# The second product of a dense FFN with slots stationary in a one-core attention, MoE and FFN kernel

## The chip, the cores and the metric

The kernel runs on one core of a Trainium2 chip. The metric is the device time of one execution in microseconds. Before and after are compared by the medians of several executions.

## The reference, cut to what matters

```python
def reference(...):
    attn_out = _attn_ref(q, k, v, omega)              # Performer features, 4 x 576 tokens, 8 heads of 64
    x = attn_out.transpose(0, 2, 1, 3).reshape(2304, 512)
    x = _moe_ref(x, expert_emb, tau, w1, w2)          # 8 experts, 512 -> 1024 -> 512
    return _moe2_ref(x, w_in, w_out)                  # the dense FFN

def _moe_ref(x, expert_emb, tau, w1, w2):
    ...
    expert_idx = np.argmax(logits, axis=1)
    gate_w = probs[np.arange(N), expert_idx]
    for e in range(E):
        mask = expert_idx == e
        h = np.maximum(x[mask] @ w1[e], 0.0)
        out[mask] = gate_w[mask, None] * (h @ w2[e])

def _moe2_ref(x, w_in, w_out):                        # 512 -> 2048 -> 512
    h = np.maximum(x @ w_in, 0.0)
    return h * h @ w_out
```

The gate is a positive number per token, and relu squared is of degree two, so the kernel applies the gate's square at the very end, to the rows of the output.

## The kernel before, in words

The work has three stages. The attention builds features of q and k, and writes the token rows x to DRAM. The MoE stage sorts the 2304 tokens by expert into 8 chunks of C = 290 slots, each of one expert: two chunks are filled from the first half of the tokens (`plan_a`), six once all tokens are there (`plan_b`). A plan builds one-hot matrices on VectorE (L726, L729, L732) and multiplies them on TensorE (L738) into a table: token numbers to gather from, token numbers to scatter to, and the gate. `gather` (L144) loads the 290 rows of a chunk by indirect DMA from GpSimd (L153) in three pieces of 128, 128 and 34 rows, transposes them on TensorE (L166) and splits them into two parts (L170, L171). Every product is done with three matmuls of split numbers (`mm3`, L185 to L189): high by high, high by low, low by high. `moe` (L252) runs a chunk: 8 blocks of hidden units, an `up` of 12 matmuls each, relu into h (ScalarE L262, VectorE L263), and with a lag of one block a `down` of 12 matmuls into four accumulators. The expert weights arrive by DMA as raw tiles (L222, L227), and `split` (L140 to L142) makes the two parts: ScalarE copies to the high part, VectorE or GpSimd subtracts for the low part. GpSimd does it for chunk 1, and for half of chunk 2. `keep` (L272) writes the chunk's result, transposed, into five column tiles yf.

The FFN (`ffn`, L306) takes the 2320 slots as NF = 5 tiles of W2 = 464 columns, and the 16 blocks of hidden units in four quarters of GF = 4. For each quarter, tile and block, `hidden` (L286) does an up of 12 matmuls, relu (L292), square (L294, L295) and a subtraction (L296) into g; two blocks later a `down` with the weights stationary and g as the moving operand adds into four accumulators of 128 outputs by 464 slots. At the end of four blocks VectorE adds them to oacc (L327, L329). In the last quarter, `finish` (L343) turns each finished chunk back: four transposes to a group of rows (L351), multiplication by the gate into an orow buffer (ScalarE L354, VectorE L356; three buffers), and an indirect scatter to the output from GpSimd (L357), 24 groups in all. The FFN's weights come as 64-bit numbers; `decode` (L104 to L118) makes them into fp32 with four operations of VectorE (L114 to L117) and splits them with GpSimd (L142). `prep_w` (L120) does it for the next quarter: the DMA (L112) and the decode go in while a quarter runs, into four buffers. A scheduler orders each engine's instructions from the traced program; each engine works strictly in that order.

Three more chunks of the kernel (`more`) run only if a token has no slot, and they do not run here. The end of the program waits for all scatters.

Of the kernel before, what the change touches and what calls it, by code (L numbers as in the profile page):

```python
# [24 lines left out]
NF, W2 = 5, 464  # L25
# [5 lines left out]
def kernel(  # L31
# [33 lines left out]
    RING, RAW, OROW = 4, 4, 1  # L65
# [3 lines left out]
    act = mctx.enter_context(tc.tile_pool(name="act", bufs=2))  # L69
# [5 lines left out]
    def columns(pool, js):  # L75
        for j in js:
            yf[j] = pool.tile([P, 2, KD, W2], F32R, name=f"yf{j}")
# [11 lines left out]
    tab = const.tile([P, 9 * (NA + NBMAX)], I32, name="tab")  # L89
    o = 0  # L90
    cuts = []
    for n in (3 * NA, 3 * NA, 3 * NA, 3 * NBMAX, 3 * NBMAX, 3 * NBMAX):
        cuts.append(tab[:, o:o + n])
        o += n
    gi_a, si_a, g2_a, gi_b, si_b, g2_b = cuts
    g2_a, g2_b = g2_a.bitcast(F32), g2_b.bitcast(F32)
# [7 lines left out]
    def decode(dst, src, kk, pool):  # L104
# [13 lines left out]
        split(dst, hi.bitcast(F32), nc.gpsimd)  # L118
# [14 lines left out]
    def cols(c):  # L133
        return (gi_a, si_a, g2_a, 3 * c) if c < NA else (gi_b, si_b, g2_b, 3 * (c - NA))

# [4 lines left out]
    def split(dst, src, eng=nc.vector):  # L140
        nc.scalar.copy(dst[:, 0], src)  # L141
        eng.tensor_sub(dst[:, 1], src, dst[:, 0].bitcast(F32))  # L142

    def gather(c, ahead=0):  # L144

        gi, _, _, col = cols(c)
        xt = act.tile([P, 2, KD, C], F32R, name="xt", tag="act")
        xT[c] = xt
        def load(t):
            n = ROWS[t][1]  # L150
            tag = dict(tag="row", bufs=2) if t < 2 or not ahead else dict(tag="orow", bufs=OROW)
            xg = s2.tile([P, DM], F32, name="xg", **tag)
            nc.gpsimd.indirect_dma_start(  # L153
                out=xg[:n], out_offset=None, in_=x_dram[:HALF] if c < NA else x_dram,
                in_offset=bass.IndirectOffsetOnAxis(ap=gi[:n, col + t:col + t + 1], axis=0),
            )
            return xg

        xgs = [load(t) for t in range(3 if ahead else 2)]
        for _ in range(ahead):  # L160
            yield
        for t, (r0, n) in enumerate(ROWS):
            xg = xgs.pop(0)
            p = px()
            for kk in range(KD):
                nc.tensor.transpose(p[:, kk * n:kk * n + n], xg[:n, kk * P:(kk + 1) * P], ident[:n, :n])  # L166
            if t == 0 and not ahead:
                xgs.append(load(2))
            pv = p[:, :KD * n].rearrange("p (k n) -> p k n", k=KD)
            nc.scalar.copy(xt[:, 0, :, r0:r0 + n], pv)  # L170
            nc.vector.tensor_sub(xt[:, 1, :, r0:r0 + n], pv, xt[:, 0, :, r0:r0 + n].bitcast(F32))  # L171
            yield
# [8 lines left out]
    def run(gen):  # L181
        for _ in gen:
            pass
# [46 lines left out]
    def feed(n):  # L230
        for _ in range(n):
# [9 lines left out]
            split(w, r, nc.gpsimd if c == 1 or (c == 2 and j) else nc.vector)  # L241
# [30 lines left out]
    def keep(c, acc):  # L272

        done = None
        for d in range(KD):
            s0 = c * C
            while s0 < (c + 1) * C:
                j, o = divmod(s0, W2)
                n = min((c + 1) * C - s0, W2 - o)
# [19 lines left out]
    def ffn_steps():  # L299

        for q0 in range(0, K2, GF):
            for j in range(NF):
                for i in range(GF):
                    yield q0, j, i

    def ffn():  # L306
        steps = list(ffn_steps())
        gs = {}
        acc = None
        for t in range(len(steps) + LAG2):  # L310
            if t:
                tick()
            if t < len(steps):
                q0, j, i = steps[t]
                gs[t] = hidden(q0 + i, yf[j])
            if t >= LAG2:
                q0, j, i = steps[t - LAG2]
                if i == 0:
                    acc = accumulators()
                down(acc, wout[q0 + i], gs.pop(t - LAG2), i, GF)  # L320
                last = None
                if i == GF - 1:
                    o = oacc[:, :, j * W2:(j + 1) * W2]
                    for d in range(KD):
                        if q0 == 0:
                            last = (nc.vector if d % 2 else nc.scalar)
                            last = last.tensor_copy(o[:, d], acc[d][:, :W2]) if d % 2 else last.copy(o[:, d], acc[d][:, :W2])  # L327
                        else:
                            last = nc.vector.tensor_add(o[:, d], o[:, d], acc[d][:, :W2])  # L329
                    if q0 == K2 - GF:  # L330
                        for c in range(NA + NB):
                            if j * W2 < (c + 1) * C <= (j + 1) * W2:
                                side.append(finish(c, oacc[:, :, c * C:(c + 1) * C]))

                q1 = q0 + GF
                if q1 < K2:
                    if j < NF - 1 and i == 1:
                        prep_w(q1 + j // 2, j % 2)
                    elif j == NF - 1 and i < GF - 2:
                        prep_w(q1 + 2 + i, 0)  # L340
                        prep_w(q1 + 2 + i, 1)
# [622 lines left out]
```

## Time and profile before

| what | value |
|---|---|
| median of 3 runs | 860.44 us |
| lowest and highest run | 854.92 and 863.81 us |
| the profiled execution | 855.59 us |
| its span, first to last instruction | 853.8 us |
| mean granted clock of TensorE | 0.985 |
| first FFN matmul | 412.23 us |
| last FFN matmul starts | 824.79 us |

All times below are in us from the start of the span. The clock is the share of full speed that TensorE was granted. Matmuls are pipelined: the duration of one overlaps the next, so what counts is how far apart their starts are. An engine that waits shows an idle time with what released it, in brackets.

### The profile page before, as it was taken

To read this page: it belongs to the slowest core of one execution; us is meant where nothing else is said; L and a number is where in the kernel's file an instruction comes from. 1 tells how busy PE (TensorE), PEld (TensorE's weight loads), DVE (VectorE), ACT (ScalarE), POOL (GpSimd) and SP (SyncE) were. 2 spreads that over 40 slices of the span, in tenths; PEclk is the share of its full clock that TensorE was granted. 3 is DMA by queue.
4 is the path that set the end of the run, shared out by engine and by line. 5 is a ranking of instruction groups with operands and counts; after the bars stand their busy time and mean duration, and the time that the engine had idled before them with its cause. 6 is when DMAs were issued, how large, how long until landed. Compare 5 with 4: busy or idle time off the path is not lost.

```text
span 853.8 us, 14040 instructions
## 1 busy us (share of the span) xinstructions
PE 812.6 (95%) x5118; PEld 750.7 (88%) x5118; DVE 511.9 (60%) x1115; ACT 361.6 (42%) x852; POOL 190.4 (22%) x217
## 2 busy tenths in 40 slices
PE   6999999998999999998999999999999999999981
PEld 6999998998989999998988888888888888888860
DVE  6777688688665788898333279333873343343430
ACT  5666787654355556554332243222322222222220
POOL 1133433533664221040000042000410011011133
PEclk9999999999999999998999999999999999999995
DMA  8334444366475776685000033000410000000111
GB/s 199 88 108 120 130 116 106 87 180 215 117 211 167 240 204 172 206 254 181 1 1 1 0 101 98 1 1 2 146 51 1 1 0 1 1 29 29 40 69 62
DMA packets 100927, 79.75 MB, mean 93 GB/s; under 512 B 29904, under 2 KB 88272, under 8 KB 100848
## 3 DMA queue, kind: packets, MB, share of 16 engines
q1 hardware_dynamic: 95728, 69.27, 28.3%
q0 software_dynamic: 5120, 9.49, 3.6%
q8 instruction: 42, 0.69, 0.3%
q14 instruction: 37, 0.30, 0.1%
HBM read 69.29 MB, written 9.47 MB: 92 GB/s over the span
## 4 chain that ended last, share of the span: by engine, by line
PE 71%; issue 14%; DVE 6%; DMA 3%; POOL 3%; ACT 1%; SPq 0%; POOLq 0%; ACTq 0%; DVEq 0%
PE pm L189 9%; PE pm L187 9%; PE pm L188 9%; PE acc L188 9%; PE acc L187 9%; PE acc L189 9%; PE pk L560 3%; DMA raw<-in_moe_w_dram 3%; PE pn L606 3%; POOL out_dram L357 2%; PE pp L537 2%; PE px L588 2%; PE pp L539 2%; PE pp L538 2%; PE px L516 2%
## 5 line engine op out<-in xcount | busy, mean ns | idle before, releaser
L292 ACT ACTIVATE r<-pm 128x464 f32<-128x464 f32 x80 | 44.7, 559 | 264.6 <-PE pm L189 264.6
L295 DVE TENSOR_TENSOR r<-r 128x464 f32<-128x464 f32 x80 | 54.8, 685 | 149.7 <-ACT r L292 149.7
L142 POOL TENSOR_TENSOR wf<-r,wf 128x512 fp32r<-128x512 f32 x32 | 51.3, 1613 | 336.7 <-ACT wf L141 310.6
L187 PE MATMUL pm<-yf,wf 128*128 128x464 f32 x320 | 120.0, 375 | 0.0
L187 PE MATMUL acc<-g,wf 128*128 128x464 f32 x320 | 119.6, 375 | 0.0
L189 PE MATMUL acc<-g,wf 128*128 128x464 f32 x320 | 119.4, 373 | 0.0
L189 PE MATMUL pm<-yf,wf 128*128 128x464 f32 x320 | 119.4, 373 | 0.0
L188 PE MATMUL pm<-yf,wf 128*128 128x464 f32 x320 | 119.2, 372 | 0.0
L188 PE MATMUL acc<-g,wf 128*128 128x464 f32 x320 | 118.9, 371 | 0.0
L141 ACT CAST wu<-raw 128x512 fp32r<-128x512 f32 x128 | 79.0, 622 | 70.2 <-PE acc L189 26.0
L142 DVE TENSOR_TENSOR wu<-raw,wu 128x512 fp32r<-128x512 f32 x104 | 82.1, 794 | 19.6 <-ACT wu L141 18.4
L187 PE MATMUL pm<-xt,wu 128*128 128x290 f32 x256 | 78.3, 306 | 2.9 <-DVE h L263 2.1
L189 PE MATMUL pm<-xt,wu 128*128 128x290 f32 x256 | 77.9, 304 | 2.5 <-DVE wu L142 2.5
L188 PE MATMUL pm<-xt,wu 128*128 128x290 f32 x256 | 76.8, 300 | 0.0
L188 PE MATMUL acc<-h,wu 128*128 128x290 f32 x256 | 71.4, 300 | 2.0 <-DVE h L263 2.0
L189 PE MATMUL acc<-h,wu 128*128 128x290 f32 x256 | 70.6, 295 | 0.0
L549 ACT ACTIVATE ft<-pp,mx 128x128 f32<-128x128 f32 x216 | 62.8, 385 | 12.6 <-DVE mx L541 12.4
L541 DVE TENSOR_REDUCE mx<-pp 128x4 f32<-128x512 f32 (+1 forms) x80 | 50.3, 631 | 29.7 <-PE pp L539 29.6
L187 PEld LDWEIGHTS acc<-g,wf 128*128 128x128 f32 x320 | 60.1, 188 | 7.9 <-DVE oacc L327 0.4
L189 PEld LDWEIGHTS acc<-g,wf 128*128 128x128 f32 x320 | 60.0, 188 | 7.4
L188 PEld LDWEIGHTS pm<-yf,wf 128*128 128x128 f32 x320 | 60.1, 188 | 7.3
L188 PEld LDWEIGHTS acc<-g,wf 128*128 128x128 f32 x320 | 60.0, 188 | 7.4
(214 smaller groups left out, 1716.2 us busy)
## 6 DMA issues: line engine op xcount, KB each, us to landing
raw<-in_moe_w_dram SPq DMA_DIRECT2D x128, 256.0 KB, 3.2
r<-in_moe_w_in_dram SPq DMA_DIRECT2D x16, 512.0 KB, 3.7
r<-in_moe_w_out_dram SPq DMA_DIRECT2D x16, 512.0 KB, 4.6
qk<-in_q_dram SPq DMA_DIRECT2D x16, 256.0 KB, 2.9
qk<-in_k_dram SPq DMA_DIRECT2D x16, 256.0 KB, 3.3
va<-in_v_dram SPq DMA_DIRECT2D x32, 128.0 KB, 3.0
x_dram<-xr SPq DMA_DIRECT2D x16, 256.0 KB, 2.6
qz<-in_q_dram SPq DMA_DIRECT2D x4, 128.0 KB, 4.0
```

The lines of the kernel that those rows point to most:

```text
L141: nc.scalar.copy(dst[:, 0], src)
L142: eng.tensor_sub(dst[:, 1], src, dst[:, 0].bitcast(F32))
L187: nc.tensor.matmul(o, lhsT=wh, rhs=xh, start=start, stop=False)
L188: nc.tensor.matmul(o, lhsT=wh, rhs=xl, start=False, stop=False)
L189: nc.tensor.matmul(o, lhsT=wl, rhs=xh, start=False, stop=stop)
L292: nc.scalar.activation(r, ph, AF.Relu, scale=2.0 ** -8)
L295: nc.vector.tensor_mul(g32, r, r)
L357: sc = nc.gpsimd.indirect_dma_start(out=out, out_offset=bass.IndirectOffsetOnAxis(ap=si[:n, col + t:col + t + 1], axis=0), in_=orow[:n], i ...
L541: nc.vector.tensor_reduce(mx[:, f0:f1], pp[:, :2 * n], axis=AX.X, op=ALU.max, negate=True)
L549: paced["exp"] = nc.scalar.activation(ft[:, f, :], pp[:, f - f0, :], AF.Exp, bias=mx[:, f:f + 1])
L560: nc.tensor.matmul(pk[:, 65 * part:65 * part + 65], lhsT=ft[:, KC[4 * part + c], :], rhs=va[:, 4 * part + c, :], start=False, stop=(part = ...
L606: nc.tensor.matmul(pn[:, t - t0, :], lhsT=qt[:, t * P:(t + 1) * P], rhs=kz[:, t // 4, :], start=True, stop=True)
```

## The change

The first product of the FFN stays as it is, but the tiles are now four of 512 slots and one of 272. For the 512-slot tiles the second product is turned over: a piece of 128 slots of g is the stationary operand, the 512 outputs of a weight block are the moving one (`down_rows`). An accumulator then holds 128 rows of the output with all 512 columns, is multiplied by the gate and added into og on VectorE (`add_rows`), and after the last quarter is scattered from there. The 272-slot tile still goes the old way, with transposes, and comes first in the last quarter. The last tile's second product is done row group by row group at the end, and each group is scattered when its sum is there. GpSimd's subtractions are done by VectorE. The gathers go by tiles of 128 slots that may cross a chunk's border, 5 and 15 loads instead of 24 of mixed size, and the tables are by those tiles. `prep_w` is placed behind the additions of the tile before.

```diff
-NF, W2 = 5, 464
+WF = (512, 512, 512, 512, (NA + NB) * C - 2048)
...
-        split(dst, hi.bitcast(F32), nc.gpsimd)
+        split(dst, hi.bitcast(F32))
...
-            split(w, r, nc.gpsimd if c == 1 or (c == 2 and j) else nc.vector)
+            split(w, r)
...
+        for (i, n), xg in zip(tiles, xgs):
+            parts = []
+            s0 = max(i * P, NA * C) if not first else i * P
+            while s0 < i * P + n:
+                o = s0 // C
+                m = min((o + 1) * C, i * P + n) - s0
+                parts.append((chunk_tile(o), s0 - o * C, s0 - i * P, m))
+                s0 += m
+            turn_rows(xg, n, parts)
+            yield
...
+    def down_rows(acc, w, g, t, f, n):
+
+        gh, gl = (g[:, k, t * P:(t + 1) * P] for k in range(2))
+        nc.tensor.matmul(acc[t], lhsT=gh, rhs=w[:, 0], start=f == 0, stop=False)
+        nc.tensor.matmul(acc[t], lhsT=gh, rhs=w[:, 1], start=False, stop=False)
+        nc.tensor.matmul(acc[t], lhsT=gl, rhs=w[:, 0], start=False, stop=f == n - 1)
+
+    def add_rows(acc, i, first):
+
+        gate = g2[:, i:i + 1]
...
+        return nc.vector.scalar_tensor_tensor(og[:, i], acc, gate, og[:, i], op0=ALU.mult, op1=ALU.add)
...
+            order = list(range(NP)) if q < NQ - 1 else [NP - 1, *range(NP - 1)]
...
+            if rows and q == NQ - 1 and o == NP - 1:
+
+                if i < GF - 1:
+                    continue
+                for r in range(KD):
+                    for k in range(GF):
+                        down_rows(acc, wout[q * GF + k], gs[t - LAG2 - GF + 1 + k], r, k, GF)
+                    add_rows(acc[r], KD * j + r, False)
+                    scatter(og[:, KD * j + r], KD * j + r)
+                continue
+            g = gs.pop(t - LAG2)
+            if rows:
+                for r in range(KD):
+                    down_rows(acc, wout[q * GF + i], g, r, i, GF)
+            else:
+                down(acc, wout[q * GF + i], g, i, GF)
...
+                if o < NP - 1 and i == GF - 1:
+                    todo = [(q1 + o // 2, o % 2)]
+                elif o == NP - 1 and i < GF - 2:
+                    todo = [(q1 + 2 + i, 0), (q1 + 2 + i, 1)]
+            for f, part in todo:
+                with tc.issue_after(pin.ins):
+                    prep_w(f, part)
```

The change moves instructions in three places. The first is VectorE near the end of the MoE chunks; wu are split expert weights, h the hidden units of a chunk, and r64 the FFN weights under decoding, here those of the second quarter. Before:

```order
L263 SCALAR_TENSOR_TENSOR h_5418<-pm_5400,h_5418 128x290
L142 TENSOR_TENSOR wu_5444<-raw_5375,wu_5444 128x512
L114 TENSOR_SCALAR r64_6255<-r64_6255 128x512
L115 SCALAR_TENSOR_TENSOR r64_6255<-r64_6255 128x512
L142 TENSOR_TENSOR wu_5462<-raw_5395,wu_5462 128x512
L116 TENSOR_SCALAR r64_6255<-r64_6255 128x512
L114 TENSOR_SCALAR r64_6396<-r64_6396 128x512
L263 SCALAR_TENSOR_TENSOR h_5465<-pm_5447,h_5465 128x290
L117 SCALAR_TENSOR_TENSOR r64_6255<-r64_6255 128x512
L115 SCALAR_TENSOR_TENSOR r64_6396<-r64_6396 128x512
```

The same place after the change:

```order
L279 SCALAR_TENSOR_TENSOR h_5434<-pm_5416,h_5434 128x290
L137 TENSOR_TENSOR wu_5451<-raw_5382,wu_5451 128x512
L137 TENSOR_TENSOR wu_5469<-raw_5411,wu_5469 128x512
L279 SCALAR_TENSOR_TENSOR h_5472<-pm_5454,h_5472 128x290
L137 TENSOR_TENSOR wu_5489<-raw_5429,wu_5489 128x512
```

The decodes of eight weights have left this place; they now stand in the FFN's first quarter.

The second is VectorE at the end of the FFN's second quarter, where the columns of the last tile are worked on; oacc and og are the sums, r2 and g belong to `hidden`. Before:

```order
L329 TENSOR_TENSOR oacc_5858<-oacc_5858,acc_7083 128x464
L116 TENSOR_SCALAR r64_7437<-r64_7437 128x512
L114 TENSOR_SCALAR r64_7578<-r64_7578 128x512
L117 SCALAR_TENSOR_TENSOR r64_7437<-r64_7437 128x512
L295 TENSOR_TENSOR r2_7215<-r2_7215 128x464
L115 SCALAR_TENSOR_TENSOR r64_7578<-r64_7578 128x512
L296 TENSOR_TENSOR g_7217<-r2_7215,g_7217 128x464
```

The same place after the change:

```order
L329 SCALAR_TENSOR_TENSOR og_5827<-acc_7053,tab_83,og_5827 128x512
L112 TENSOR_SCALAR r64_7164<-r64_7164 128x512
L112 TENSOR_SCALAR r64_7208<-r64_7208 128x512
L112 TENSOR_SCALAR r64_7217<-r64_7217 128x512
L112 TENSOR_SCALAR r64_7257<-r64_7257 128x512
L113 SCALAR_TENSOR_TENSOR r64_7164<-r64_7164 128x512
L311 TENSOR_TENSOR r2_7185<-r2_7185 128x272
L113 SCALAR_TENSOR_TENSOR r64_7208<-r64_7208 128x512
L113 SCALAR_TENSOR_TENSOR r64_7217<-r64_7217 128x512
L113 SCALAR_TENSOR_TENSOR r64_7257<-r64_7257 128x512
L114 TENSOR_SCALAR r64_7164<-r64_7164 128x512
L312 TENSOR_TENSOR g_7187<-r2_7185,g_7187 128x272
```

Four weights are decoded side by side behind the additions, and the operations that make g stand between them, one after every few.

The third is TensorE at the border of chunks 1 and 2; pm and acc are the sums of `up` and `down`, px the transposed rows xg. Before:

```order
L187 MATMUL pm_3586<-xt_2841,wu_3536 128x290
L188 MATMUL pm_3586<-xt_2841,wu_3536 128x290
L166 MATMUL px_3404<-ident_78,xg_3356 128x128 x4
L187 MATMUL acc_3383<-h_3557,wu_3554 128x290
L187 MATMUL acc_3384<-h_3557,wu_3554 128x290
L187 MATMUL acc_3385<-h_3557,wu_3554 128x290
L187 MATMUL acc_3386<-h_3557,wu_3554 128x290
L188 MATMUL acc_3383<-h_3557,wu_3554 128x290
```

After the change:

```order
L204 MATMUL acc_3371<-h_3631,wu_3610 128x290
L205 MATMUL acc_3371<-h_3631,wu_3610 128x290
L153 MATMUL px_3390<-ident_78,xg_3341 128x128 x4
L153 MATMUL px_3435<-ident_78,xg_3343 128x128 x4
L153 MATMUL px_3481<-ident_78,xg_3345 128x128 x4
L153 MATMUL px_3753<-ident_78,xg_3705 128x128 x4
L203 MATMUL pm_3684<-xt_3389,wu_3628 128x290
L203 MATMUL pm_3711<-xt_3389,wu_3648 128x290
```

The transposes stood one group at a time between the matmuls of chunk 1; now all four groups stand together behind chunk 1's last matmul and ahead of chunk 2's first.

## Rows read from the trace of the kernel before

**Rows 1.** The page's first part: busy time of each engine, share of the span, instructions.

```profile
PE 812.6 (95%) x5118; PEld 750.7 (88%) x5118; DVE 511.9 (60%) x1115; ACT 361.6 (42%) x852; POOL 190.4 (22%) x217
```

**Rows 2.** The windows: stretch, length, busy time (instructions) of each engine, clock, DMA share, GB/s.

```profile
core 0: us, PE busy (x) PEld busy (x) DVE busy (x) ACT busy (x) POOL busy (x), PEclk, DMA share, GB/s
186.00:411.00 225.00, 215.85 (x1585) 211.20 (x1584) 174.41 (x364) 116.08 (x256) 70.48 (x54) 0.98 0.65 192
...
380.00:395.00 15.00, 12.26 (x67) 11.36 (x66) 15.00 (x32) 7.11 (x20) 3.98 (x2) 0.77 0.71 226
...
613.00:714.00 101.00, 101.00 (x480) 89.71 (x479) 52.06 (x85) 26.36 (x46) 10.60 (x7) 1.00 0.08 24
...
714.00:825.00 111.00, 111.00 (x555) 98.05 (x554) 42.97 (x70) 27.73 (x47) 14.35 (x14) 1.00 0.07 25
...
825.00:853.80 28.80, 6.99 (x41) 4.73 (x39) 4.49 (x7) 3.43 (x5) 10.34 (x10) 0.67 0.21 76
```

**Rows 3.** Timeline of TensorE: start us, us, engine, line, operation, out<-in, shape.

```profile
205.60 0.29 PE L189 MATMUL pm<-xt,wu 128*128 128x290 f32 x1
...
208.41 0.29 PE L189 MATMUL pm<-xt,wu 128*128 128x290 f32 x1
...
412.23 0.37 PE L187 MATMUL pm<-yf,wf 128*128 128x464 f32 x1
...
814.63 0.37 PE L187 MATMUL pm<-yf,wf 128*128 128x464 f32 x1
...
818.84 0.37 PE L189 MATMUL acc<-g,wf 128*128 128x464 f32 x1
...
819.69 0.37 PE L188 MATMUL acc<-g,wf 128*128 128x464 f32 x1
...
824.79 0.37 PE L189 MATMUL acc<-g,wf 128*128 128x464 f32 x1
```

**Rows 4.** Timeline of GpSimd in the tail; in brackets the idle time before.

```profile
839.81 0.98 POOL L357 DMA_INDIRECT out_dram<-orow,tab  x1 [0.30 <-issue]
843.71 1.09 POOL L357 DMA_INDIRECT out_dram<-orow,tab  x1 [2.91 <-ACT orow L354]
```

**Rows 5.** The waits, 825.00 to the end: us in total, times, longest.

```profile
ACT orow L354 <- DMA out_dram<-orow,tab: 12.7, 3, 5.3
```

**Rows 6.** The waits of TensorE in the MoE stretch, 186 to 411.

```profile
PE pm L189 <- DVE wu L142: 2.5, 4, 0.9
PE pm L187 <- DVE h L263: 2.1, 2, 1.8
```

**Rows 7.** Timeline of TensorE near the end of the MoE chunks.

```profile
388.56 0.45 PE L187 MATMUL pm<-xt,wu 128*128 128x290 f32 x1
...
390.50 0.45 PE L189 MATMUL pm<-xt,wu 128*128 128x290 f32 x1
```

**Rows 8.** Timeline of VectorE and GpSimd: operations on weights, beside each other and alone.

```profile
389.37 0.68 DVE L142 TENSOR_TENSOR wu<-raw,wu 128x512 fp32r<-128x512 f32 x1
389.97 0.42 DVE L114 TENSOR_SCALAR r<-r 128x512 uint32<-128x512 uint32 x1
...
393.30 0.68 DVE L115 SCALAR_TENSOR_TENSOR r<-r 128x512 uint32<-128x512 uint32 x1
...
498.68 1.31 POOL L142 TENSOR_TENSOR wf<-r,wf 128x512 fp32r<-128x512 f32 x1 [3.72 <-ACT wf L141]
...
498.69 1.58 DVE L114 TENSOR_SCALAR r<-r 128x512 uint32<-128x512 uint32 x1 [3.23 <-DMA r<-in_moe_w_in_dram]
```

**Rows 9.** The groups by line: busy time, mean ns, idle time before.

```profile
L329 DVE TENSOR_TENSOR oacc<-oacc,acc 128x464 f32<-128x464 f32 x60 | 36.8, 632 | 45.7 <-PE acc L189 45.7
```

**Rows 10.** The groups of VectorE, 203 to 229.

```profile
L732 DVE TENSOR_TENSOR zhr<-i,zps 128x384 f32<-128x384 f32 x6 | 3.0, 545 | 0.0
```

**Rows 11.** Timeline of TensorE around the second routing table.

```profile
223.52 4.25 PE L738 MATMUL px<-zhc,zhr 128*128 128x90 f32 x36
...
232.87 0.60 PE L166 MATMUL px<-ident,xg 128*128 128x128 f32 x4
```

More of the change, by code (lines that the diff above doesn't have):

```diff
@@ L138, in expert, with split @@
         return nc.sync.value_load(t[0:1, i:i + 1], min_val=0, max_val=E - 1)
-    def split(dst, src, eng=nc.vector):
+    def split(dst, src):
         nc.scalar.copy(dst[:, 0], src)
-        eng.tensor_sub(dst[:, 1], src, dst[:, 0].bitcast(F32))
-    def gather(c, ahead=0):
[L146 to L159, printed above, removed]
+        nc.vector.tensor_sub(dst[:, 1], src, dst[:, 0].bitcast(F32))
@@ L160, in gather, with chunk_tile @@
+    def chunk_tile(c):
+        if c not in xT:
+            xT[c] = act.tile([P, 2, KD, C], F32R, name="xt", tag="act")
+        return xT[c]
+    def gather(c, ahead=0):
+        first = c < NA
+        i0 = -(-c * C // P) if c != NA else c * C // P
+        i1 = -(-(c + 1) * C // P)
+        end = NA * C if first else (NA + NB) * C
+        tiles = [(i, min(P, end - i * P)) for i in range(i0, i1)]
+        xgs = [load_rows(i, n, first) for i, n in tiles]
         for _ in range(ahead):
             yield
-        for t, (r0, n) in enumerate(ROWS):
[L163 to L172, printed above, removed]
+        for (i, n), xg in zip(tiles, xgs):
[8 more added lines that the diff above has]
+            yield
@@ L297, in hidden, with scatter @@
         return g
[L299 to L304, printed above, removed]
[L306 to L307 removed]
+    def down_rows(acc, w, g, t, f, n):
[5 more added lines that the diff above has]
+        gate = g2[:, i:i + 1]
+        if first:
+            if i % 2:
+                nc.scalar.activation(og[:, i], acc, AF.Copy, scale=gate)
+            return nc.vector.tensor_scalar(og[:, i], acc, gate, None, ALU.mult) if not i % 2 else None
+        return nc.vector.scalar_tensor_tensor(og[:, i], acc, gate, og[:, i], op0=ALU.mult, op1=ALU.add)
+    def scatter(rows, i, n=P, only=True):
+        sc = nc.gpsimd.indirect_dma_start(
+            out=out, out_offset=bass.IndirectOffsetOnAxis(ap=si[:n, i:i + 1], axis=0),
+            in_=rows, in_offset=None, bounds_check=T - 1, oob_is_err=False,
+        )
+        if only:
+            tc.declare_no_dep(sc.ins, group="out", reason="a token has one slot: the rows differ")
+            tc.add_to_no_dep_group("out", sc.ins)
+    def ffn():
+        NQ, NP = K2 // GF, len(WF)
+        steps = []
+        for q in range(NQ):
+            order = list(range(NP)) if q < NQ - 1 else [NP - 1, *range(NP - 1)]
+            steps += [(q, o, j, i) for o, j in enumerate(order) for i in range(GF)]
         gs = {}
         acc = None
+        pin = None
         for t in range(len(steps) + LAG2):
@@ L313, in ffn @@
             if t < len(steps):
[L314 to L341, printed above, removed]
```

180 lines of the change are left out of this document (108 added, 72 removed).

## The prediction

> **What bounds the kernel now.** The first view is the page's table of engines: TensorE is busy 95% of the span and VectorE 60% [rows 1]. So I looked for the stretches in which TensorE is not fully fed. The second view cuts the span into stages [rows 2]. In a middle quarter of the FFN (613 to 714) TensorE is busy for all 101.00 us; nothing can be won there unless the matmuls themselves get cheaper. Three stretches differ. The MoE chunks (186 to 411) leave 225.00 - 215.85 = 9.15 us idle. The last quarter takes 111.00 where the others take 101.00. And the tail from 825.00 to the end has only 6.99 us of TensorE work in 28.80 us. The third view is the timeline of TensorE [rows 3], from which spacings are taken, because a matmul's own duration overlaps the next one.
>
> Why is the tail long? ScalarE waits 12.7 us for the scatters out of the three orow buffers [rows 5]: transpose, copy, scatter and then wait for the buffer's transfer. The last scatter starts at 843.71 [rows 4], 10.1 us before the end of the span; this is what one scatter costs when nothing is behind it.
>
> **The product itself: no change.** The 464-column matmuls start (818.84 - 814.63) / 20 = 0.2105 us apart, the 290-column ones (208.41 - 205.60) / 21 = 0.1338 [rows 3]. No row has 512 or 272 columns, so I draw a line through the two: 0.00044 us a column, 0.2317 for 512 and 0.1259 for 272. A quarter is now 384 matmuls of 512 and 96 of 272: 89.0 + 12.1 = 101.1 us; before it was 480 x 0.2105 = 101.0. The number of weight loads is the same too: one per matmul, of slots instead of weights. If the 290-column spacing is already the floor that a weight load sets, 272 columns cost 0.1338 and the FFN 384 x 0.0079 = 3.0 us more; the other end is 0. I take 0, because the line through both sizes has nearly no fixed part (0.006 us), as it would not if a load set the smaller one.
> On this the Trainium skill ("TensorE: Matmul & The Clock Gate", LDWEIGHTS) gives a load 128 columns over 1.2 GHz, 107 ns, which is less than either spacing: by it 0, by the other reading 3.0. No run here shows 272 columns yet.
>
> **Transposes leave the last quarter.** The FFN runs from 412.23 to 825.00 (the last matmul's 824.79 plus one spacing) [rows 3], 412.8 us, of which 1920 x 0.2105 = 404.2 is product. The other 8.6 us are transposes between matmuls and what they cost around them: between 818.84 and 819.69 stand two spacings (0.42) and one group of four transposes, 0.43. After the change three groups are left (272 slots): 1.3. Gain 7.3.
>
> **The tail.** Rows go to the scatter from the accumulated sums, so no buffer is waited for. The last 12 matmuls fill one row tile; then an addition on VectorE (0.632 at 464 columns [rows 9], so 0.70 at 512), a start of GpSimd of about 0.3 (its gap between two scatters [rows 4]), 0.16 for the matmul's end beyond its spacing, and 10.1 as before: 11.3 us instead of 28.8. The scatters of the earlier row tiles are 12 matmuls, 2.8 us, apart, and one takes 1.09 [rows 4]: they don't queue. The last scatter now has 128 rows instead of 34; bounds for this: 0 to 2 us. Gain 17.5.
>
> **Quarter borders.** VectorE now decodes the next quarter's weights inside the FFN. At a border (second order block of the change) 16 decode operations, one subtraction and four operations for hidden stand in a row before the first of the last four weights is ready. Alone, a decode operation takes 0.42 or 0.68 [rows 8]. Counted from the end of tile 3's products: additions 0.7, decode 8 x 0.42 + 8 x 0.68 + 0.68 = 9.5, hidden 4 x 0.4, so 11.8 us. TensorE reaches the up that needs this weight after six ups and downs of the 272-column tile (12 matmuls, 1.5 us each) and two ups of 512 (2.8 each): 14.6 us. The slack is 2.8 us; for the subtraction of the third 272-column unit, behind nine decode operations, it is about 2. At the last border two 272-column tiles follow each other, their steps are half as long, and I expect a stall of 1 to 2 us. The loads have landed: each takes the buffer of a weight decoded tiles earlier. Bounds: 0, or 6 us at each of three borders if the burst runs at the mean of contended and free. Loss 1.5.
>
> **GpSimd's subtractions.** 56 of them go to VectorE at 0.68 each [rows 8], 38 us in all. What they cost GpSimd is seen in the pair at 498.7: the GpSimd subtraction takes 1.31, and VectorE's L114, which starts 0.01 later, 1.58, against 0.42 when alone at 389.97 [rows 8]. So each brings VectorE 0.68 and saves it up to 1.16: about even, and in the FFN VectorE has 52.06 busy of 101.00 [rows 2], which covers it.
> The Trainium skill ("SBUF — State Buffer", Who interferes with whom) says the same of the place: GpSimd and VectorE share one pair of ports, and the second to come is blocked for the whole instruction. The trace nearly agrees: 1.31 and 0.42 one after the other would be 1.73, measured were 1.58. If every one of the 56 collided, the rule would make 56 x (1.31 - 0.68) = 35 us of VectorE's time come free, against none by the even reckoning; neither is on the path outside the MoE stretch.
>
> **MoE.** TensorE's waits there [rows 6] are for VectorE's wu and h. VectorE is busy 15.00 of 15.00 us from 380 to 395 [rows 2], because the order before has eight decodes there (first order block); the clock is 0.77 in that stretch, and the matmuls at 388.56 to 390.50 are 0.2425 apart [rows 7], 0.109 more than 0.1338; 24 of them, 2.6 us. Lost in all: 9.15 + 2.6 = 11.8 us. The decodes leave this place. Two new waits come in. First, in chunk 1 the six one-hot builds of 0.545 [rows 10] and some others, 7.3 us of VectorE, stand between two h; TensorE has about 3.2 us of work (24 x 0.1338) and a little queue: a loss of some 3 (0 to 5). Second, at the border of chunks 1 and 2 all transposes of the gathered rows stand in one place on TensorE (third order block), 34 matmuls after the table is made, 4.6 us. Before, 9.35 us pass from the table's first matmul (223.52) to the first transpose (232.87) [rows 11], 5.1 of these after its last. Four tiles with two buffers of PSUM and about 1.4 us for copy and subtraction follow. TensorE stands for some 4.5 us (1 to 8), perhaps with 1.3 for a lower clock afterwards. Net: 11.8 - 3.0 - 5.8 = 3.0 gained, between a loss of 3 and a gain of 10.
>
> **The sum.** 853.8 - 7.3 - 17.5 + 1.5 - 3.0 = 827.5 us of span. The profiled execution took 855.59, that is 1.8 around its span: 829.3. It lay 4.85 below the median of 860.44, near the lowest of three runs; a median of the changed kernel should lie above its good runs too. I put 2.7 on top: 832.
>
> **Rivals.**
> - The MoE gain comes whole: the gathered rows land in time, and no bubble takes the place of the old waits. For it: the plan starts with fewer operations, and GpSimd no longer has subtractions before its gathers. Against it: the order of TensorE above. 8.8 less: 823.
> - The border of chunks 1 and 2 and the plan cost more than they free: 5 + 8 + 2.6 for the clock instead of 8.8, and 2 of the old loss stays. About 9 more: 841.
> - VectorE is late at each quarter border by 6 us, with operations at 0.66 to 0.79 on the mean and loads that land after the burst has begun. 16.5 more: 848.
> - Slower: the same burst at contended prices. If each of its 17 operations takes 1.55 as beside GpSimd, it is 26.4 + 0.7 + 1.6 = 28.7 against 14.6 us of cover, a stall of 14 at the first weight, 1 or 2 more at the next; three borders, 45 us, less the 1.5 counted: 875. It decides from 9.5 us of stall a border ((860.4 - 832) / 3), which is an operation of about 1.3. For it: VectorE works strictly in order, and 1.58 has been seen. Against it: the GpSimd operations beside which it was seen are gone.
> - The change doesn't do what it says where the slots' load sets the spacing: 835.
>
> **How the numbers follow.** My forecast has 0.52 (with the load case, which lies in its own range of 825 to 840), the whole MoE gain 0.18, the dearer chunk border 0.13, the late borders 0.11, the slow one 0.06. A measurement of this kernel can tell about 1%, 8.6 us: faster is below 851.8, slower above 869.0. The first three cases are faster, and half of the fourth: 0.88. Same: the other half and a part of the slow one, 0.07. Slower 0.05. The range of 817 to 848 leaves out a gain beyond the whole MoE case with a shorter last landing, and the slow side.
>
> **What would show it.** Right: full 101 us windows in all four quarters, a tail of 11 to 12 us after the last matmul with scatters only, spacings of 0.232 and 0.126, no VectorE-bound stretch before the FFN. Wrong: TensorE idle before a 272-column tile or before a quarter's third weight, waiting for g or wf2; a gap of over 8 us between chunks 1 and 2; 512-column matmuls more than 0.24 apart; a last scatter that starts more than 2 us after the last product.

## The result and the profile after

The changed kernel takes 821.26 us (median of 4 runs, 820.91 to 824.46); the kernel before, measured beside it, takes 857.68 (852.1 to 863.81). The ratio is 0.958, with a 95% interval of 0.951 to 0.966: faster by 4.2%. The profiled execution took 820.91 us, with this first part of its page (busy time, share of the span, instructions):

```profile
span 819.0 us, 13678 instructions
...
PE 793.1 (97%) x5018; PEld 714.6 (87%) x5018; DVE 500.8 (61%) x1153; ACT 356.9 (44%) x847; POOL 95.9 (12%) x152
```

The span is 34.8 us shorter. To see where, cut both spans at the same four events of TensorE: the first matmul of chunk 1, the first matmul of the FFN, the end of the last product, the end of the span.

| stretch | before | after | gained | forecast |
|---|---|---|---|---|
| start to chunk 1 | 203.36 | 201.52 | 1.8 | 0 |
| chunks 1 to 7 | 208.87 | 200.46 | 8.4 | 3.0 |
| FFN | 412.77 | 406.85 | 5.9 | 7.3 - 1.5 = 5.8 |
| tail | 28.80 | 10.17 | 18.6 | 17.5 |

These are the windows of the kernel after for chunk 1, chunk 7, the FFN and the tail (columns as in [rows 2]):

```profile
201.52:242.55 41.03, 35.48 (x268) 34.07 (x267) 31.36 (x97) 18.31 (x43) 5.60 (x6) 0.95 0.57 168
376.23:401.98 25.75, 25.75 (x194) 25.75 (x193) 15.44 (x28) 12.85 (x27) 0.00 (x0) 1.00 0.46 134
401.98:808.83 406.85, 406.85 (x1946) 339.18 (x1944) 202.82 (x355) 115.84 (x207) 17.69 (x18) 1.00 0.11 37
808.83:819.00 10.17, 0.15 (x1) 0.00 (x0) 0.75 (x1) 0.00 (x0) 1.56 (x2) 0.66 0.20 74
```

And this is chunk 7 in the kernel before:

```profile
380.06:412.23 32.17, 29.43 (x194) 28.52 (x193) 25.77 (x51) 13.88 (x32) 3.92 (x2) 0.89 0.50 155
```

Chunk 7 shrank from 32.17 to 25.75 us. VectorE's busy time in it went from 25.77 to 15.44 with the decodes gone, and the clock from 0.89 to 1.00. 25.75 is 192 matmuls at 0.134: nothing is lost there any more. Chunk 1 went the other way, from 37.15 to 41.03. Its end on the timeline of TensorE:

```profile
235.31 0.63 PE L153 MATMUL px<-ident,xg 128*128 128x128 f32 x4
237.57 0.63 PE L153 MATMUL px<-ident,xg 128*128 128x128 f32 x4 [1.64 <-DMA xg<-x_dram,tab]
240.83 2.07 PE L153 MATMUL px<-ident,xg 128*128 128x128 f32 x8 [2.63 <-DMA xg<-x_dram,tab]
242.55 0.83 PE L203 MATMUL pm<-xt,wu 128*128 128x290 f32 x2
```

The gathers that it waits for stand on GpSimd:

```profile
231.95 1.01 POOL L143 DMA_INDIRECT xg<-x_dram,tab  x1 [50.02 <-DVE tab L858]
233.26 1.35 POOL L143 DMA_INDIRECT xg<-x_dram,tab  x1 [0.30 <-issue]
234.92 1.01 POOL L143 DMA_INDIRECT xg<-x_dram,tab  x1 [0.30 <-PE acc L205]
```

That is the bubble of the third order block: the third tile is asked for 3.0 us after the first, its transposes start 5.9 us later, and TensorE has nothing else in its order meanwhile. Which part of the change brought this order is seen below, where both parts are tried on the kernel before. In the tail, the answer to [rows 4, 5]: the last matmul, its addition, its scatter, and no wait for a buffer.

```profile
808.59 0.39 PE L320 MATMUL acc<-wf,g 128*128 128x512 f32 x1
```

```profile
809.01 0.75 DVE L329 SCALAR_TENSOR_TENSOR og<-acc,tab,og 128x512 f32<-128x512 f32 x1 [2.05 <-PE acc L320]
```

```profile
810.04 0.98 POOL L332 DMA_INDIRECT out_dram<-og,tab  x1 [0.64 <-DVE og L329]
```

How long this scatter is on its way, and what moves after it has landed:

```profile
DMA to landing us min/median/max: 3.6/3.6/3.6
```

```profile
814.20:819.00 4.80, 0.00 (x0) 0.00 (x0) 0.00 (x0) 0.00 (x0) 0.00 (x0) 0.50 0.00 0
```

So the last transfer has landed 5.3 us before the span ends, and in the last 4.8 of them the profile shows no engine busy and no DMA.

The FFN is full: TensorE is busy for all 406.85 us, and no start at a quarter border lies more than 0.15 beyond its spacing.

### The profile page after: what moved, and what is told of

The parts are those of the page before. It is cut to its first block, busy times and chain, and to the rows that moved or that the text cites. A ratio compares the mean times of both kernels' runs of the same rounds, so it can differ in the third digit from the quotient of the medians.

```text
span 819.0 us, 13678 instructions
## 1 busy us (share of the span) xinstructions
PE 793.1 (97%) x5018; PEld 714.6 (87%) x5018; DVE 500.8 (61%) x1153; ACT 356.9 (44%) x847; POOL 95.9 (12%) x152
## 4 chain that ended last, share of the span: by engine, by line
PE 92%; DVE 4%; DMA 1%; ACT 1%; issue 0%; SPq 0%; POOLq 0%; POOL 0%; ACTq 0%
PE pm L203 12%; PE pm L205 12%; PE pm L204 12%; PE acc L319 7%; PE acc L320 7%; PE acc L318 7%; PE acc L204 5%; PE acc L203 5%; PE acc L205 5%; PE pk L608 3%; PE pn L654 3%; PE px L636 2%; PE pp L585 2%; PE pp L587 2%; PE pp L586 2%; PE px L564 2%
## 5 line engine op out<-in xcount | busy, mean ns | idle before, releaser
L308 ACT ACTIVATE r<-pm 128x512 f32<-128x512 f32 (+1 forms) x80 | 44.7, 560 | 250.6 <-PE pm L205 250.6
L311 DVE TENSOR_TENSOR r<-r 128x512 f32<-128x512 f32 (+1 forms) x80 | 51.2, 640 | 134.8 <-ACT r L308 134.6
L203 PE MATMUL pm<-yf,wf 128*128 128x512 f32 (+1 forms) x320 | 119.0, 372 | 0.0
L205 PE MATMUL pm<-yf,wf 128*128 128x512 f32 (+1 forms) x320 | 119.0, 372 | 0.0
L204 PE MATMUL pm<-yf,wf 128*128 128x512 f32 (+1 forms) x320 | 118.7, 371 | 0.0
L137 DVE TENSOR_TENSOR wu<-raw,wu 128x512 fp32r<-128x512 f32 x128 | 87.7, 689 | 36.9 <-ACT wu L136 34.5
L319 PE MATMUL acc<-wf,g 128*128 128x512 f32 x256 | 101.2, 395 | 0.0
L318 PE MATMUL acc<-wf,g 128*128 128x512 f32 x256 | 100.8, 395 | 0.0
L320 PE MATMUL acc<-wf,g 128*128 128x512 f32 x256 | 100.5, 395 | 0.0
L203 PE MATMUL pm<-xt,wu 128*128 128x290 f32 x256 | 77.7, 304 | 0.0
L205 PE MATMUL pm<-xt,wu 128*128 128x290 f32 x256 | 76.5, 299 | 0.0
L204 PE MATMUL pm<-xt,wu 128*128 128x290 f32 x256 | 76.3, 298 | 0.0
L203 PEld LDWEIGHTS pm<-yf,wf 128*128 128x128 f32 x320 | 60.1, 188 | 10.9 <-ACT r L308 0.2
L204 PEld LDWEIGHTS pm<-yf,wf 128*128 128x128 f32 x320 | 60.1, 188 | 10.8
L205 PEld LDWEIGHTS pm<-yf,wf 128*128 128x128 f32 x320 | 60.1, 188 | 10.6
L329 DVE SCALAR_TENSOR_TENSOR og<-acc,tab,og 128x512 f32<-128x512 f32 x48 | 34.6, 745 | 44.3 <-PE acc L320 44.3
L320 PEld LDWEIGHTS acc<-wf,g 128*128 128x128 f32 x256 | 48.1, 188 | 11.6
```

Source lines behind the costliest of these rows:

```text
L137: nc.vector.tensor_sub(dst[:, 1], src, dst[:, 0].bitcast(F32))
L203: nc.tensor.matmul(o, lhsT=wh, rhs=xh, start=start, stop=False)
L204: nc.tensor.matmul(o, lhsT=wh, rhs=xl, start=False, stop=False)
L205: nc.tensor.matmul(o, lhsT=wl, rhs=xh, start=False, stop=stop)
L308: nc.scalar.activation(r, ph, AF.Relu, scale=2.0 ** -8)
L311: nc.vector.tensor_mul(g32, r, r)
```

## The experiments

The theory after the result: the turned product and the tail did what the forecast says; what came on top (5.4 us in chunks 1 to 7) is the placement of the decodes, which freed VectorE there. The main rival: it is GpSimd's subtractions, whose leaving freed VectorE. Two runs undo one part of the change, two do one part alone on the kernel before.

**Subtractions back on GpSimd.**

```diff
-        split(dst, hi.bitcast(F32))
+        split(dst, hi.bitcast(F32), nc.gpsimd)
...
-            split(w, r)
+            split(w, r, nc.gpsimd if c == 1 or (c == 2 and j) else nc.vector)
```

> The changed kernel with the 56 subtractions back on GpSimd, nothing else. Theory (the placement of the decodes is what freed the MoE stretch, the subtractions are about even for VectorE): 821 to 826 us against 821, chunk 7 stays at 25.7 to 26 us, what is lost is lost in chunks 1 and 2, where gathers queue behind subtractions. Rival (GpSimd's subtractions slowed VectorE, and their leaving is the larger part): 828 us or more, lost in every chunk with a decode and at the quarter borders.

Measured 826.61 us (823.62 to 827.82), ratio to before 0.965 (0.960 to 0.970): between the ranges of theory and rival. Chunk 7 takes 26.33, 0.3 above the theory's range. From chunk 1 to the FFN it is 203.8 us against 200.5, and the loss is spread over chunks 2, 3, 4, 6 and 7 (1.2, 0.5, 0.6, 0.4, 0.6). Chunk 1 is as long as in the changed kernel (41.1 us), but by another wait: no transpose waits for its rows there, and TensorE waits for an h instead.

```profile
223.72 0.61 PE L204 MATMUL acc<-h,wu 128*128 128x290 f32 x1 [5.16 <-DVE h L279]
```

The FFN with the tail is 417.3 against 417.0, with 0.8 lost at the last border. That GpSimd subtracts in the FFN again costs so little because few operations of a decode meet a subtraction: of the 24 first operations of a decode on VectorE, 400 to 790, three take 1.36, 0.93 and 0.63 us, the others 0.42.

```profile
L112 DVE TENSOR_SCALAR r<-r 128x512 uint32<-128x512 uint32 x24 | 11.0, 489 | 5.0 <-DMA r<-in_moe_w_out_dram 5.0
```

**Decodes early again.**

```diff
-                if o < NP - 1 and i == GF - 1:
+                if o < NP - 1 and i == 1:
...
-                with tc.issue_after(pin.ins):
-                    prep_w(f, part)
+                prep_w(f, part)
```

> The changed kernel with the decodes traced where they were before, without the order behind the additions; the subtractions stay on VectorE. Theory (placement): eight weights are decoded in chunks 5 to 7 again, chunk 7 takes 30 to 33 us instead of 25.75, the kernel 826 to 830 us. Rival (the subtractions on GpSimd made the old loss): chunk 7 within 1 us of 25.75, the kernel 820 to 823 us.

Measured 826.88 us (825.34 to 828.58), ratio 0.966 (0.961 to 0.970), in the theory's range. Chunk 7 is at 29.69, 0.3 below the theory's range, and chunk 6 at 27.66, together 5.9 us over the changed kernel:

```profile
380.06:409.75 29.69, 27.24 (x181) 26.00 (x181) 23.22 (x45) 13.98 (x29) 0.00 (x0) 0.94 0.49 144
```

VectorE has 23.22 us of work in that chunk again. The rival's numbers did not come. That chunk 7 is shorter than the 32.17 before is no sign for it: here six decodes begin in chunk 6 and two in chunk 7, before four and four. Both chunks together take 57.4 us, against 58.4 before and 51.5 in the changed kernel.

**The two parts alone, on the kernel before.** The first moves the subtractions only:

```diff
-        split(dst, hi.bitcast(F32), nc.gpsimd)
+        split(dst, hi.bitcast(F32))
...
-            split(w, r, nc.gpsimd if c == 1 or (c == 2 and j) else nc.vector)
+            split(w, r)
```

> The kernel before with only the subtractions moved to VectorE. Theory (placement): chunk 2 gains 1 to 3 us, chunk 7 and its neighbours lose as much, since VectorE has more to do there: 854 to 862 us against 857.7. Rival (subtractions): 846 to 851 us, chunk 7 near 27 us.

Measured 849.13 us (848.76 to 852.06) against 854.87 measured beside it, ratio 0.994 (0.991 to 0.997). The rival was nearer here: the time is in its range, chunk 2 takes 27.27 (29.82 before), chunk 7 29.08 (32.17), though not the rival's 27. Chunk 6 gives back 1.5 (27.75 against 26.21). Why does it gain, though VectorE gets more work? The groups of VectorE between 400 and 790 in the kernel before, for the first and the last operation of a decode:

```profile
L114 DVE TENSOR_SCALAR r<-r 128x512 uint32<-128x512 uint32 x16 | 13.1, 819 | 6.7 <-DMA r<-in_moe_w_in_dram 6.5
L117 DVE SCALAR_TENSOR_TENSOR r<-r 128x512 uint32<-128x512 uint32 x16 | 13.0, 814 | 0.2
```

And with the subtractions moved:

```profile
L117 DVE SCALAR_TENSOR_TENSOR r<-r 128x512 uint32<-128x512 uint32 x16 | 11.0, 686 | 0.1
L114 DVE TENSOR_SCALAR r<-r 128x512 uint32<-128x512 uint32 x16 | 6.8, 427 | 13.8 <-DMA r<-in_moe_w_in_dram 9.4 <-DMA r<-in_moe_w_out_dram 2.8 <-SPq L914 1.5
```

L114 falls from 819 to 427 ns: six of the sixteen before, which start while GpSimd subtracts, take 1.34 to 1.58 us, the other ten 0.41 to 0.43. One of these ten also runs beside a subtraction, but starts 0.01 us ahead of it, and there the subtraction is the longer one (1.60, against 1.31 in [rows 8], where it was first):

```profile
600.02 0.43 DVE L114 TENSOR_SCALAR r<-r 128x512 uint32<-128x512 uint32 x1 [3.23 <-DMA r<-in_moe_w_in_dram]
```

```profile
600.03 1.60 POOL L142 TENSOR_TENSOR wf<-r,wf 128x512 fp32r<-128x512 f32 x1 [3.73 <-ACT wf L141]
```

VectorE's busy time over the span falls from 511.9 to 507.5 us, with 56 subtractions more on it.

The second moves the decodes only:

```diff
-                    if j < NF - 1 and i == 1:
-                        prep_w(q1 + j // 2, j % 2)
+                    if j < NF - 1 and i == GF - 1:
+                        todo = [(q1 + j // 2, j % 2)]
...
+                    for f, part in todo:
+                        with tc.issue_after(pin[0].ins):
+                            prep_w(f, part)
```

> The kernel before with only the decodes placed behind the additions of the FFN's tiles; the subtractions stay on GpSimd. Theory (placement): chunk 7 falls from 32.17 to 26 us or so, the whole to 849 to 853 us. Rival (subtractions): chunk 7 above 30 us, the whole 855 to 860 us; if the bursts stall at the quarter borders the FFN grows above 412.8 us.

Measured 847.94 us (847.17 to 852.34), ratio 0.993 (0.989 to 0.997): a little more gain than forecast. Chunk 1 and chunk 7:

```profile
201.94:243.31 41.37, 37.60 (x252) 36.29 (x251) 26.52 (x64) 14.87 (x31) 25.76 (x22) 0.88 0.44 127
380.57:406.96 26.39, 26.20 (x192) 25.96 (x193) 16.19 (x33) 13.22 (x32) 0.00 (x0) 1.00 0.41 130
```

Chunk 7 falls to 26.39 us. GpSimd does nothing in it (0.00): the subtractions of these weights leave the chunk together with their decodes, so this row alone does not tell the two theories apart. Chunk 1 loses 4.2 us (41.37 against 37.15) at a granted clock of 0.88, where it was 1.00 before; why was not tried. From the FFN's first matmul to the end it is 440.9 against 441.6 before, so the bursts stall nothing.

**Both parts, on the kernel before** (the two diffs above together).

> The kernel before with both of the moves that can be made alone: subtractions on VectorE, decodes behind the additions. Alone they gave 849.1 and 847.9 against 854.9. Theory (both relieve the same stretch of VectorE, in part): chunk 7 near 25.8 us, 843 to 847 us. Rival (they are independent): 841 to 843 us. The FFN and the tail are as before: 441 us from its first matmul to the end of the span; what is left to 821 us is the turned product, the tail and the transposes.

Measured 846.4 us (843.87 to 848.55) against 853.25 measured beside it, ratio 0.990 (0.985 to 0.995), in the theory's range. From the FFN on nothing changes (441.1). Chunks 1 to 7 of these profiles, in us:

| kernel | chunk 1 | 2 to 5 | 6 and 7 | 1 to 7 |
|---|---|---|---|---|
| before | 37.15 | 113.34 | 58.38 | 208.87 |
| subtractions moved | 37.47 | 109.69 | 56.83 | 204.00 |
| decodes moved | 41.37 | 110.71 | 52.94 | 205.02 |
| both moved | 38.03 | 110.51 | 52.09 | 200.63 |
| changed kernel | 41.03 | 107.97 | 51.47 | 200.46 |

In chunks 6 and 7 the decodes' place does most of it: 5.4 us alone, against 1.6 for the subtractions and 6.3 for both. In chunks 1 to 5 only the subtractions gain (3.3). So the first theory holds for the end of the MoE chunks and the rival for their beginning. Over chunks 1 to 7 the gains of 4.9 and 3.9 nearly add up (8.2 for both), against the theory; the medians are too rough to tell.

Both moves together reach the 200.5 of the changed kernel, but in sum only. The rest of the change, the gathers by tiles, makes chunk 1 3.0 us longer and the others 3.2 shorter. And the order of the bubble comes with the subtractions: with them on VectorE the kernel before too has its transposes together behind chunk 1's last matmul, three groups instead of four, and waits for their rows:

```profile
240.13 0.63 PE L166 MATMUL px<-ident,xg 128*128 128x128 f32 x4 [1.78 <-DMA xg<-x_dram,tab]
```

In both runs with GpSimd subtracting they stand between matmuls, and none waits.

**The product not turned.** The sums of all tiles stand by columns (od is a list of five), the branch for the last tile goes, half of the first quarter's copies go to VectorE, and there are three orow buffers.

```diff
-            rows = j < NP - 1
+            rows = False
...
-                        pin = nc.vector.tensor_add(od[:, d], od[:, d], acc[d][:, :WF[j]])
+                        pin = nc.vector.tensor_add(od[j][:, d], od[j][:, d], acc[d][:, :WF[j]])
...
-                    side.append(finish(od, KD * j, WF[j]))
+                    side.append(finish(od[j], KD * j, WF[j]))
```

> The changed kernel with the second product of all tiles as it was before (weights stationary, sums by columns), so all 19 row groups go through transposes and orow buffers again; tiles, tables, decodes and subtractions as in the changed kernel. Theory (the turned product gains nothing by itself, its worth is the transposes and the tail): matmul spacing of the second product 0.230 instead of 0.233, last quarter 5 to 6 us longer (12 more groups of 0.43), tail 16 to 19 us instead of 10.2, together 832 to 836 us against 821. Rival (most of the old tail came from chunk-wise finishing and its pieces of 34 rows, which are gone here too): tail under 13 us, 824 to 828 us.

Measured 832.7 us (830.44 to 833.12), ratio 0.974 (0.969 to 0.979). Time, tail and spacing are the theory's. Its FFN and its tail:

```profile
404.85:814.35 409.50, 409.50 (x1990) 343.31 (x1989) 201.05 (x357) 121.63 (x216) 13.73 (x14) 1.00 0.10 34
814.35:831.10 16.75, 3.23 (x21) 2.08 (x19) 0.89 (x2) 3.44 (x5) 4.92 (x5) 0.69 0.25 96
```

The turned product is thus worth 409.50 - 406.85 = 2.7 us in the FFN and 16.75 - 10.17 = 6.6 in the tail. The other 12 us of the tail (28.80 to 16.75) are gained without turning, which is the rival's point: 5 groups are left after the last product instead of 10 [rows 2], since groups are now whole tiles of 128 rows and none waits for a chunk that ends in the last tile. The size of the groups and their order were not tried apart. The 2.7 is less than 11 groups of 0.43 because the turned matmul is the slower one, as these two pairs of rows show, the first of the kernel after, the second of this run:

```profile
411.92 0.39 PE L318 MATMUL acc<-wf,g 128*128 128x512 f32 x1
...
413.09 0.39 PE L319 MATMUL acc<-wf,g 128*128 128x512 f32 x1
```

```profile
811.82 0.40 PE L204 MATMUL acc<-g,wf 128*128 128x512 f32 x1
...
814.12 0.39 PE L205 MATMUL acc<-g,wf 128*128 128x512 f32 x1
```

(413.09 - 411.92) / 5 = 0.234 and (814.12 - 811.82) / 10 = 0.230. Over the 750 spacings of each the means are 0.2333 and 0.2301.

**The last tile in the common order.**

```diff
-            if rows and q == NQ - 1 and o == NP - 1:
-
-                if i < GF - 1:
-                    continue
...
-                continue
```

> The changed kernel with the last tile's second product in the order of the other tiles (all four row groups of one block, then the next block), so the four sums are finished 0.7 us apart. Theory (the tail is one addition, one scatter and its landing; scatters start 1.3 us apart): the last scatter starts 3 us after the last product instead of 1.2, the kernel 822 to 824 us. Rival (the transfers overlap and only the last product counts): 820.5 to 821.5 us. Second rival (four transfers side by side land later): 825 us or more.

Measured 825.47 us (822.98 to 825.96), ratio 0.967 (0.962 to 0.971); from the FFN's first matmul to the end it is 419.0 against 417.0. Four scatters queue on GpSimd; the last product starts at 808.72, and the last scatter at 812.65:

```profile
811.36 0.98 POOL L332 DMA_INDIRECT out_dram<-og,tab  x1 [0.31 <-issue]
812.65 0.98 POOL L332 DMA_INDIRECT out_dram<-og,tab  x1 [0.30 <-issue]
```

So the first theory's mechanism holds: grouping the last tile by rows is worth 2.0 us. The last scatter starts 3.9 us after the last product's start, against 1.45, and the span ends 8.4 us after that start, against 8.9, so the second rival's late landing is not seen. But the median, 4 us higher, lies in that rival's range, and these 2.0 don't cover it; the profiled execution took 822.98. Kernels with the same code up to there begin the MoE chunks up to 3 us apart: at 169.3 here and in the changed kernel, at 171.9 in the run with early decodes. The granted clock differs before that (the changed kernel, then the run with early decodes):

```profile
130.00:168.00 38.00, 35.75 (x326) 34.29 (x325) 27.96 (x97) 27.32 (x92) 15.87 (x23) 1.00 0.33 94
```

```profile
130.00:168.00 38.00, 36.98 (x324) 35.61 (x322) 26.63 (x93) 26.71 (x89) 13.72 (x21) 0.96 0.32 90
```

Of the ten profiles of the changed kernel and its variants, five show 0.96 there and begin at 170.8 to 171.9, five show 1.00 and begin at 168.9 to 169.3. So medians of four runs say less than stretches of one profile. Whether this is all of the 4 us is open.

**The bubble between chunks 1 and 2.** Four runs try to shorten it. The first two put the matmuls of the routing table earlier, by an order behind them on a down of chunk 1 (TABF is 4, then 3):

```diff
+                    tabled[0] = nc.tensor.matmul(pt[:, :na * ncol], lhsT=hr[:, j, :], rhs=hc[:, j].rearrange("p a c -> p (a c)"), start=(i + j == 0), stop=(i + j == n - 1))
...
+                if c == NA - 1 and f - LAG == TABF:
+                    with tc.issue_after(tabled[0].ins):
+                        down(acc, wd, hs.pop(f - LAG), f - LAG, K1)
```

> The changed kernel with the matmuls of the second routing table put 24 matmuls earlier on TensorE (they stand before the fifth down of chunk 1). Theory (the bubble between chunks 1 and 2 is the time from the table to the third gathered tile, less the matmuls left): the gathers start 2.5 to 3 us earlier, TensorE's wait for xg falls from 4.3 to under 2 us, the half clock after it goes, the kernel 817 to 819.5 us. Rival (the loads of weights that run beside the gathers, or VectorE's one-hot builds, set the landing): the wait moves to the table's matmuls, the kernel 820.5 to 822 us.

> The changed kernel with the matmuls of the second routing table 38 matmuls earlier than in the changed kernel (both halves together, before the fourth down of chunk 1). Times of stretches are counted from the first matmul of chunk 1, since the start of the MoE stage lies up to 2.5 us apart from run to run. In the run with 24 matmuls the table ended 2.1 us earlier and chunk 1 was 2.3 us shorter. Theory (chunk 1 ends with the landing of three gathers, which follows the table): TensorE waits some 2 us for VectorE at the table, chunk 1 takes 37.5 to 39 us against 41.0, the wait for xg is under 1 us. Rival (the landing follows the loads of weights beside it, not the table): chunk 1 40 to 41.5 us, a landing of over 7 us. The whole: 817 to 822 us by both, given back in part where h waits.

With 24 matmuls: 821.2 us (818.66 to 822.56), chunk 1 38.70, but chunks 2 and 3 give 2.4 us back. The wait for xg is 2.2 instead of 4.3, the lower clock stays. The first theory failed for the whole; the time is in the rival's range. With 38: 821.15 us (817.99 to 821.54), chunk 1 39.72, between the two theories, chunks 1 to 7 198.2 against 200.5. The wait for xg is gone, and another has come:

```profile
221.08 0.58 PE L205 MATMUL pm<-xt,wu 128*128 128x290 f32 x1 [2.88 <-DVE h L281]
224.17 4.29 PE L787 MATMUL px<-zhc,zhr 128*128 128x92 f32 x36
```

Before the table TensorE waits 2.88 us for an h, which stands on VectorE behind the one-hot builds. So with the earlier table a part of the bubble moves to another place, where TensorE's work is used up again.

The third gives the gathered rows a fourth buffer, the fourth joins it with TABF = 3, beside the changed kernel itself:

```diff
-        xgs = [load_rows(i, n, first) for i, n in tiles]
+        xgs = [load_rows(i, n, first, bufs=4) for i, n in tiles]
```

> The changed kernel with four buffers for gathered rows instead of three, so that the load of chunk 3's first tile doesn't wait for a transpose. Theory (the third tile's landing sets the end of the bubble): no change, chunk 1 within 0.7 us of 41.0, chunks 2 and 3 together within 1 us of 54.5, the kernel 820 to 824 us. Rival (the fourth group of transposes, which stands before chunk 2's first matmul, waits for its buffer): chunk 1 at least 1.5 us shorter, 819 to 821 us.

> The changed kernel with the table 38 matmuls earlier and four buffers for gathered rows, both together. From chunk 1's first matmul to the FFN's the changed kernel took 200.5 us, the two edits alone 198.2 and 198.7. Theory (they act on the same bubble): 197.5 to 198.5 us, the kernel 0.2 to 0.4% below the changed kernel of the same call, 818 to 820 us. Rival (they add up): 196.5 us. Second rival (what is won at the border is lost where h waits): 199.5 us or more, no difference.

> The changed kernel once more, unaltered, beside the version with both edits: 820 to 823 us, 200 to 201 us from chunk 1 to the FFN, 417 us from the FFN's first matmul to the end.

The fourth buffer alone: 820.88 us (818.84 to 823.35), chunk 1 40.15 (0.9 shorter), chunks 1 to 7 198.7; between the two theories. Half of the 0.9 can be chance: in the two runs on the product and the last tile, which have the same code there as the changed kernel, chunk 1 takes 40.6. Both edits: 819.57 us (817.5 to 822.61), ratio to before 0.959 (0.956 to 0.962); the changed kernel beside it 820.6 (819.53 to 823.89), 0.960 (0.958 to 0.963). Chunks 1 to 7 take 197.3 against 200.7 us, nearer the theory than its rival, so 3 us are saved there in the profiles, but the intervals overlap: that this version beats the changed kernel is not shown.

## Why the prediction was right, and where it was not

The measured 821.3 lies in the range (817 to 848), on the side forecast, but 11 us below the 832 given and near the range's lower end. Of these, 8.5 are in the sum itself (827.5 of span against 819.0), 2.7 were put on top because the profiled execution before lay below its median; after, it lies only 0.35 below, so that was not needed.

- *The product itself: no change.* Right. 768 x 0.2302 + 768 x 0.2333 + 384 x 0.1258 = 404.3 us against 404.2. The line through two sizes gave 0.2317 and 0.1259; 272 columns are not held up by weight loads: the profile shows a load for 0.188 us, but two matmuls, each with its load, start 0.1258 apart. That the turned form costs 0.003 more a matmul was not foreseen, nor visible before.
- *Transposes leave the last quarter.* The FFN lost 5.9, forecast 5.8, but that is luck: two errors cancel. Of the 8.6 us put down to transposes, 1.6 are 12 matmuls of the last MoE chunk (acc<-h), which stand behind the FFN's first matmul in both kernels and stay. So the term was about 6 and not 7.3, and the borders took less than was set against it.
- *Quarter borders.* Forecast a loss of 1.5, measured below 0.4. The slower rival, the burst at contended prices, did not come; even with GpSimd subtracting again the last border loses 0.8, and the operation that was seen at 1580 ns takes 489 on the mean.
- *The tail.* 18.6 for 17.5. The mechanism was told too simply: only 6.6 come from rows that go straight to the scatter, 12 from fewer groups after the last product. The span ends 8.9 us after the start of the last scatter, of 128 rows, not 10.1. Nor is that what one scatter costs: it lands after 3.6 us (4.0 before), and the other 5.3 (6.1 before) pass after it, at the end of the program. The earlier scatters of the last tile do queue, at 805.85, 807.14 and 808.42, against the forecast; the last one doesn't wait for them.
- *GpSimd's subtractions.* "About even" for VectorE was the step that hid a gain: they free 4.4 us of VectorE's time (far from the 35 of the reckoning in which every one collides), and alone they are worth 0.6% (0.3 to 0.9).
- *MoE.* Here the sum failed. The new losses came to 8.7 us, forecast 8.8, again with two errors that cancel: 7.1 us at the border (forecast 5.8) and 1.6 of waits for h (forecast 3.0). What was mis-sized is the old loss, "lost in all: 11.8", read as span minus busy time plus the lower clock. A matmul of 290 columns is shown busy for 0.30 us but starts every 0.134, so a gap of up to 0.17 us after it is not seen, and a longer one is seen 0.17 short. Counted as what each start lies beyond its spacing, chunks 1 to 7 lost 18.1 us before (6.1 in chunk 1, 2.9 in 2, 6.4 in 7) and 11.7 after. That is 6.4 gained, and about 2 from fewer transposes of gathered rows (72 and 60 in this stretch): 8.4. By the runs it is the sum of what the two moves gain, 4.9 and 3.9 alone; the prediction had the subtractions at about even, and so at nothing here. Its reason for the busy stretch from 380 to 395 was also misread: four of the eight decodes begin there, the other four in chunks 5 and 6. The Trainium skill ("Perfetto Trace Analysis", Identifying the Most-Contended Engine) says that matmul busy time does not tell how close a kernel is to its limit, because matmuls are pipelined. The trace agrees: 9.15 us idle from 186 to 411 [rows 2] against 18.1 by starts in chunks 1 to 7. But the page has pipelined matmuls look smaller in a trace, and in this profile they are shown longer (0.30) than their spacing (0.134).
- *Rivals.* The time fell on "the MoE gain comes whole" (823), but not its mechanism: the bubble it excluded is there. The likeliest case had the new waits right in sum and too small an old one; the result lies in the range because the range reached past the case of the whole gain.
- The 1.8 us before chunk 1 were in no term, and are within what kernels with the same code differ by there.

## What to carry to other kernels

Measure what a stretch loses from the starts of its matmuls against their free spacing, not from busy time. Before pricing an operation that moves off an engine, look at what it does to the neighbour: here VectorE took over 56 subtractions, and its own operations got shorter by more than these take. Where work for a later stage can be done in either of two, put it in the one whose other engine has time: the decodes cost 5 to 6 us in the last two MoE chunks and nothing that was measured in the FFN. And before putting an idle tail down to its last transfer, see when that transfer landed: here 5.3 of 8.9 us came after it.

## What the runs showed of the hardware that was not expected

- A 512-column matmul starts every 0.2333 us where the activations are stationary and the weights move, and every 0.2301 where it is the other way round; same shapes, same three products, 1.4%. The cause was not tried.
- In the FFN of the kernel before, a VectorE operation with one input (L114) takes 1.34 to 1.58 us in the six of 16 cases in which it starts while GpSimd subtracts, and 0.41 to 0.43 in the others; where it started 0.01 us ahead, the subtraction took 1.60 instead of 1.31. With the subtractions gone the mean of all 16 falls from 819 to 427 ns.
- Transposes that wait for three gathers asked for within 3 us start 3.4, 4.3 and 5.9 us after the gathers begin; what holds the third was not separated.
- After the last scatter has landed, the program takes 5.3 us more (6.1 before the change); in the last 4.8 of these the profile shows no engine busy and no DMA.
- Profiles of kernels with the same code up to there differ by up to 3 us in where the MoE chunks begin, and the late ones show a granted clock of 0.96 instead of 1.00 between 130 and 168 us.
